# Single-query attention over 256 heads: a tile's maximum, weights and values are placed beside the next tile's product

## The chip, the cores and the metric

One NeuronCore of a Trainium2 chip. The metric is the time of one launch on the device in microseconds (us), as the median of several runs. TensorE is called PE here (its weight loads PEld), VectorE DVE, ScalarE ACT, GpSimd POOL and SyncE SP.

## What is computed

Eight batches of 32 heads, each with a single query row of 128 numbers, 4096 keys and 4096 values, all in bf16. Softmax is taken in full over the 4096 keys of each head.

```python
B, H, Sq, Skv, Dh = 8, 32, 1, 4096, 128
def reference(q, k, v):
    scale = q.shape[-1] ** -0.5
    scores = jnp.einsum('bhqd,bhkd->bhqk', q, k) * scale
    attn = _softmax(scores, axis=-1)
    return jnp.einsum('bhqk,bhkd->bhqd', attn, v)
```

K and V are 256 x 4096 x 128 x 2 bytes each, 537 MB together, and every byte of them is used once.

## The kernel before

The 256 heads go through the core in 64 tiles of four heads (G = 4). A tile of K or V is 128 partitions x 128 keys (C) x 128 numbers of d, 4 MB; 32 partitions hold one head. K and V tiles share one pool of five buffers (`kv_pool`, SLOTS = 5), and SP issues their loads (line 106), one transfer a tile, in the order k(t+1), v(t). A load waits until the tile that was in its buffer has been read for the last time. The last v alone is loaded in four pieces.

The work on tile t is in two functions. `scores_of(t)` first forms the product of K and the query on DVE, in place, in chunks of MC = 64 keys: a multiplication by the query (line 132), then an addition of the upper half of d onto the lower half (line 135), so two of each per tile. PE then sums the remaining 64 numbers of d into four per key, by 16 multiplications with the identity that accumulate in one PSUM bank `ps` (line 144). DVE reduces these four to one score (line 149), takes the maximum of the partition (line 153), spreads it over 32 columns (line 155), takes the extreme over the 32 partitions of the head (line 160) and adds it to a mask that keeps each head on its own partitions (line 164, `bias`). ACT forms the weights with four exponentials (line 170), one per head, with their sums; PE adds the sums over the partitions (`zp`, line 175), and DVE takes the reciprocal (`rz`, line 177).

`values_of(t)` multiplies the weights by V on PE, 32 multiplications into one PSUM bank `av` (line 187). ACT copies the result out (`comb`, line 192), PE puts the four parts of it together (`op`, line 195), and ACT scales it by `rz` (line 202). Eight tiles' results go out in one store (line 206).

Every fourth tile `q_prep` loads four tiles' queries from POOL (line 115), spreads them over the partitions on PE (line 117) and copies them on ACT (line 121).

The main loop calls `scores_of(t)`, then `values_of(t - 1)`. The kernel text gives no engine order by hand beyond the order of these calls: the instructions of an engine are put into a fixed stream when the program is built, and each engine works through its stream strictly in order. That stream need not be the order of the calls, as the rows below show. The score bank `ps`, the bank `av` and the weights `w` have two buffers each.

Of the kernel before, what the change touches and what calls it, by code (L numbers as in the profile page):

```python
# [11 lines left out]
F32 = mybir.dt.float32  # L12
# [7 lines left out]
def kernel(  # L20
# [10 lines left out]
    P = nc.NUM_PARTITIONS  # L31
# [3 lines left out]
    C = S // PH  # L35
    NT = NH // G
# [1 line left out]
    UC = 128  # L38
    DS = 512 // UC
    NU = C // UC  # L40
    MC = 64
    QN = 512 // D
    ON = 8
    CB = 4
# [10 lines left out]
    small = ctx.enter_context(tc.tile_pool(name="small", bufs=3))  # L55
# [40 lines left out]
    loads = {}  # L96

    def load(kind, t):
        src = k_t if kind == "k" else v_t
        buf = kv_pool.tile([P, C, D], BF16, name=f"{kind}t", tag="kv")  # L100
        cuts = [C]
        if kind == "v" and t == NT - 1:
            cuts = [C // 2, C // 4, C // 8, C // 8]
        c0 = 0
        for n in cuts:
            nc.sync.dma_start(buf[:, c0 : c0 + n, :], src[t, :, c0 : c0 + n, :])
            c0 += n
        loads[kind, t] = buf
# [3 lines left out]
    def q_prep(t):  # L112
        if t % QN == 0:
            qrow = q_pool.tile([G, QN, D], BF16, name="qrow", tag="qrow")
            nc.gpsimd.dma_start(qrow[:], q_g[:, t : t + QN, :])  # L115
            qp = ps_q.tile([P, QN * D], F32, name="qp", tag="qp")
            nc.tensor.matmul(  # L117
                qp[:], lhsT=sel[:], rhs=qrow.rearrange("g n d -> g (n d)"), start=True, stop=True
            )
            qb = q_pool.tile([P, QN, D], BF16, name="qb", tag="qb")  # L120
            nc.scalar.activation(out=qb.rearrange("p n d -> p (n d)"), in_=qp[:], func=ACT.Copy)  # L121
            qbs[t // QN] = qb

    state = {}

    def scores_of(t):
        kt = loads.pop(("k", t))
        qb = qbs[t // QN]
        j = t % QN
        for c0 in range(0, C, MC):  # L130
            part = kt[:, c0 : c0 + MC, :]
            nc.vector.tensor_tensor(  # L132
                out=part, in0=part, in1=qb[:, j : j + 1, :].to_broadcast([P, MC, D]), op=ALU.mult
            )
            nc.vector.tensor_tensor(  # L135
                out=part[:, :, 0 : D // 2], in0=part[:, :, 0 : D // 2],
                in1=part[:, :, D // 2 : D], op=ALU.add,
            )
        sc = small.tile([P, C], F32, name="sc", tag="sc")
        for u in range(NU):  # L140
            ps = ps_s.tile([P, UC, DS], F32, name="ps", tag="ps")
            n = D // 2 // DS
            for s in range(n):
                nc.tensor.matmul(  # L144
                    ps[:], lhsT=ident[:],
                    rhs=kt[:, u * UC : (u + 1) * UC, s * DS : (s + 1) * DS],
                    start=(s == 0), stop=(s == n - 1),
                )
            nc.vector.tensor_reduce(  # L149
                out=sc[:, u * UC : (u + 1) * UC], in_=ps[:], axis=AX.X, op=ALU.add  # L150
            )
        pmax = small.tile([P, 1], F32, name="pmax", tag="pmax")
        nc.vector.tensor_reduce(out=pmax[:], in_=sc[:], axis=AX.X, op=ALU.max)  # L153
        spread = small.tile([P, 32], F32, name="spread", tag="spread")
        nc.vector.tensor_scalar(  # L155
            out=spread[:], in0=zero[:], scalar1=pmax[:, 0:1], scalar2=-scale,
            op0=ALU.add, op1=ALU.mult,
        )
        nmax = small.tile([P, 1], F32, name="nmax", tag="nmax")
        nc.vector.tensor_reduce(  # L160
            out=nmax[:], in_=spread[:], axis=AX.X, op=ALU.min, apply_transpose=True
        )
        bias = small.tile([P, G], F32, name="bias", tag="bias")
        nc.vector.tensor_scalar(  # L164
            out=bias[:], in0=own[:], scalar1=nmax[:, 0:1], scalar2=None, op0=ALU.add
        )
        w = w_pool.tile([P, C, G], BF16, name="w", tag="w")
        esum = small.tile([P, G], F32, name="esum", tag="esum")
        for g in range(G):
            nc.scalar.activation(  # L170
                out=w[:, :, g], in_=sc[:], func=ACT.Exp, bias=bias[:, g : g + 1], scale=scale,
                accum_out=esum[:, g : g + 1],
            )
        zp = ps_z.tile([G, 1], F32, name="zp", tag="zp")
        nc.tensor.matmul(zp[:], lhsT=esum[:], rhs=ones[:], start=True, stop=True)  # L175
        rz = small.tile([G, 1], F32, name="rz", tag="rz")
        nc.vector.reciprocal(out=rz[:], in_=zp[:])  # L177
        state[t] = (w, rz)
# [3 lines left out]
    def values_of(t):  # L182
        w, rz = state.pop(t)
        vt = loads.pop(("v", t))
        av = ps_v.tile([CB * G, CB * D], F32, name="av", tag="av")
        for c0 in range(0, C, CB):
            nc.tensor.matmul(  # L187
                av[:], lhsT=w[:, c0 : c0 + CB, :], rhs=vt[:, c0 : c0 + CB, :],
                start=(c0 == 0), stop=(c0 == C - CB),
            )  # L190
        comb = small.tile([CB * G, CB * D], BF16, name="comb", tag="comb")
        nc.scalar.activation(out=comb[:], in_=av[:], func=ACT.Copy)  # L192
        op = ps_o.tile([G, D], F32, name="op", tag="op")
        for m in range(CB):
            nc.tensor.matmul(  # L195
                op[:], lhsT=ident[0 : CB * G, m * G : (m + 1) * G],
                rhs=comb[:, m * D : (m + 1) * D], start=(m == 0), stop=(m == CB - 1),
            )
        if t % ON == 0:
            stages[t // ON] = o_pool.tile([G, ON, D], BF16, name="stage", tag="stage")  # L200
        stage = stages[t // ON]
        nc.scalar.activation(out=stage[:, t % ON, :], in_=op[:], func=ACT.Copy, scale=rz[:, 0:1])  # L202
        if t == NT - 1 or t == NT - 2 or (t % ON == ON - 1):
            lo = {NT - 1: NT - 1, NT - 2: NT - ON}.get(t, t - ON + 1)
            eng = nc.scalar if t == NT - 1 else nc.gpsimd
            eng.dma_start(o_g[:, lo : t + 1, :], stage[:, lo % ON : t % ON + 1, :])
# [3 lines left out]
    for t in range(NT):  # L210
        if t + 1 < NT:
            load("k", t + 1)
        load("v", t)
        if t + 2 < NT:
            q_prep(t + 2)
        scores_of(t)
        if t > 0:
            values_of(t - 1)
    values_of(NT - 1)


# [28 lines left out]
```

## Time and profile before

| what | value |
|---|---|
| median of 3 runs | 1506.79 us (1506.4 to 1508.59) |
| the profiled execution, its own time | 1508.7 us |
| its span, first to last instruction | 1506.9 us |
| mean granted TensorE clock | 0.766 of full speed |
| DVE busy | 953.6 us, 63% of the span |
| PE busy | 893.4 us, 59% |
| K and V read | 537 MB, 356 GB/s over the span |

The profiled execution is 1.9 us longer than the median, and 1.8 us of its time lie outside the span. The profile page gives shares over the whole span; a stage's limit is read from the timeline and from what each engine waited for. Durations are in microseconds unless marked ns. Two neighbouring instructions of one engine can overlap by some ten ns in the records, and the ends of matrix multiplications are modelled.

### The profile page before, as it was taken

The numbers are of one execution on the slowest core, as the hardware profiler recorded it, in microseconds if no ns is written. First come the engines' busy times: TensorE is split into PE (matmuls) and PEld (weight loads), VectorE is DVE, ScalarE is ACT, GpSimd is POOL, SyncE is SP. The second block draws the span as 40 slices with busy tenths as digits, with TensorE's granted clock in tenths as the row PEclk, the third lists the DMA queues.
The fourth block names the chain that finished last, engine by engine and source line by source line (L and its number), as shares of the span: only waits on it lengthen the run. The fifth ranks groups of instructions, "written<-read, shape, count | busy, mean of one in ns | idle before, by whom it ended". The sixth has DMA issues, their size and how long they took to land.

```text
span 1506.9 us, 8736 instructions
## 1 busy us (share of the span) xinstructions
PE 893.4 (59%) x3472; PEld 326.9 (22%) x3472; DVE 953.6 (63%) x642; ACT 182.2 (12%) x657; POOL 15.7 (1%) x36
## 2 busy tenths in 40 slices
PE   2656556566475574665745647556566565564666
PEld 0212222122121221221212212222122122221222
DVE  6575675665756756657566576575665766756653
ACT  0111011111010110111101101011011110110111
POOL 1000000000000000000000000000000000000000
PEclk9777777787786876878778678687787787777878
DMA  9999898888988988889898898898888888888870
GB/s 403 431 432 392 352 378 354 379 347 349 391 336 361 376 348 377 355 342 389 329 383 362 335 402 344 341 392 346 376 361 347 379 350 358 378 349 377 348 321 1
DMA packets 19681, 537.58 MB, mean 357 GB/s; under 512 B 2776, under 2 KB 2844, under 8 KB 3128
## 3 DMA queue, kind: packets, MB, share of 16 engines
q1 hardware_dynamic: 18864, 536.88, 85.2%
q8 instruction: 27, 0.44, 0.1%
q0 software_dynamic: 768, 0.14, 0.1%
q14 instruction: 14, 0.11, 0.0%
q10 hardware_dynamic: 8, 0.00, 0.0%
HBM read 536.94 MB, written 0.07 MB: 356 GB/s over the span
## 4 chain that ended last, share of the span: by engine, by line
DVE 63%; PE 27%; ACT 7%; issue 1%; DMA 1%; ACTq 0%; DVEq 0%
DVE kt L132 37%; PE ps L144 25%; DVE kt L135 19%; ACT w L170 7%; DVE sc L149 3%; DVE pmax L153 1%; DVE spread L155 1%; DVE bias L164 1%; DVE nmax L160 1%; PE zp L175 1%; DMA kt<-in_k_dram 1%; PE av L187 1%; DVE rz L177 0%; ACTq L170 0%; PE op L195 0%
## 5 line engine op out<-in xcount | busy, mean ns | idle before, releaser
L144 PE MATMUL ps<-kt,ident 128*128 128x512 bf16 x1024 | 383.9, 554 | 473.2 <-DVE kt L135 473.2
L132 DVE TENSOR_TENSOR kt<-kt,qb 128x8192 bf16<-128x8192 bf16 x128 | 560.3, 4419 | 12.9 <-DMA kt<-in_k_dram 12.6
L187 PE MATMUL av<-vt,w 128*16 128x512 bf16 x2048 | 481.3, 384 | 0.0
L144 PEld LDWEIGHTS <-ident 128*128 128x128 bf16 x1024 | 132.8, 130 | 719.4 <-issue 701.3
L135 DVE TENSOR_TENSOR kt<-kt 128x4096 bf16<-128x4096 bf16 x128 | 287.1, 2283 | 0.0
L149 DVE TENSOR_REDUCE sc<-ps 128x128 f32<-128x512 f32 x64 | 44.2, 691 | 380.6 <-PE ps L144 380.6
L187 PEld LDWEIGHTS <-w 128*16 128x16 bf16 x2048 | 173.8, 90 | 325.8 <-issue 105.0
L170 ACT ACTIVATE w<-sc,bias 128x128 bf16<-128x128 f32 x256 | 110.8, 567 | 999.2 <-DVE bias L164 999.2
L177 DVE RECIPROCAL rz<-zp 4x1 f32<-4x1 f32 x64 | 9.9, 155 | 135.3 <-PE zp L175 135.3
L170 ACT ACTIVATION_READ_ACCUMULATOR w<-sc,bias 128x1 f32 x256 | 64.7, 253 | 0.0
L192 ACT ACTIVATE comb<-av 16x512 bf16<-16x512 f32 x64 | 37.6, 587 | 223.7 <-PE av L187 223.7
L117 PE MATMUL qp<-qrow,sel 4*128 4x512 bf16 x16 | 9.3, 583 | 83.5 <-ACT qb L121 68.2
L195 PE MATMUL op<-comb,ident 16*4 16x128 bf16 x256 | 24.2, 212 | 42.5 <-ACT comb L192 42.5
L195 PEld LDWEIGHTS <-ident 16*4 16x4 bf16 x256 | 16.8, 77 | 70.0 <-issue 70.0
L202 ACT ACTIVATE stage<-op,rz 4x128 bf16<-4x128 f32 x64 | 22.9, 358 | 30.0 <-PE op L195 30.0
L153 DVE TENSOR_REDUCE pmax<-sc 128x1 f32<-128x128 f32 x64 | 18.3, 286 | 2.1
L175 PE MATMUL zp<-ones,esum 128*4 128x1 f32 x128 | 12.3, 165 | 11.1 <-ACT w L170 11.0
L121 ACT ACTIVATE qb<-qp 128x512 bf16<-128x512 f32 x16 | 9.6, 597 | 68.3 <-DVE kt L132 58.8
L115 POOL DMA_DIRECT2D qrow<-in_q_dram x16 | 9.3, 581 | 798.9 <-PE qp L117 798.9
L155 DVE TENSOR_SCALAR spread<-zero,pmax 128x32 f32<-128x32 f32 x64 | 15.4, 241 | 2.3
L164 DVE TENSOR_SCALAR bias<-own,nmax 128x4 f32<-128x4 f32 x64 | 14.6, 229 | 2.4
L175 PEld LDWEIGHTS zp<-ones,esum 128*4 128x4 f32 x128 | 5.8, 84 | 43.6 <-ACT w L170 43.6
(18 smaller groups left out, 23.3 us busy)
## 6 DMA issues: line engine op xcount, KB each, us to landing
kt<-in_k_dram SPq DMA_DIRECT2D x64, 4096.0 KB, 15.0
vt<-in_v_dram SPq DMA_DIRECT2D x63, 4096.0 KB, 12.3
vt<-in_v_dram SPq DMA_DIRECT2D x1, 2048.0 KB, 10.1
vt<-in_v_dram SPq DMA_DIRECT2D x1, 1024.0 KB, 12.2
vt<-in_v_dram SPq DMA_DIRECT2D x2, 512.0 KB, 13.4
qrow<-in_q_dram POOLq DMA_DIRECT2D x16, 4.0 KB, 6.5
out_dram<-stage POOLq DMA_DIRECT2D x7, 8.0 KB, 6.6
out_dram<-stage POOLq DMA_DIRECT2D x1, 7.0 KB, 2.0
```

What stands on the lines that cost most here:

```text
L132: nc.vector.tensor_tensor(out=part, in0=part, in1=qb[:, j : j + 1, :].to_broadcast([P, MC, D]), op=ALU.mult)
L135: nc.vector.tensor_tensor(out=part[:, :, 0 : D // 2], in0=part[:, :, 0 : D // 2], in1=part[:, :, D // 2 : D], op=ALU.add,)
L144: nc.tensor.matmul(ps[:], lhsT=ident[:], rhs=kt[:, u * UC : (u + 1) * UC, s * DS : (s + 1) * DS], start=(s == 0), stop=(s == n - 1),)
L149: nc.vector.tensor_reduce(out=sc[:, u * UC : (u + 1) * UC], in_=ps[:], axis=AX.X, op=ALU.add)
L153: nc.vector.tensor_reduce(out=pmax[:], in_=sc[:], axis=AX.X, op=ALU.max)
L155: nc.vector.tensor_scalar(out=spread[:], in0=zero[:], scalar1=pmax[:, 0:1], scalar2=-scale, op0=ALU.add, op1=ALU.mult,)
L164: nc.vector.tensor_scalar(out=bias[:], in0=own[:], scalar1=nmax[:, 0:1], scalar2=None, op0=ALU.add)
L170: nc.scalar.activation(out=w[:, :, g], in_=sc[:], func=ACT.Exp, bias=bias[:, g : g + 1], scale=scale, accum_out=esum[:, g : g + 1],)
L175: nc.tensor.matmul(zp[:], lhsT=esum[:], rhs=ones[:], start=True, stop=True)
L187: nc.tensor.matmul(av[:], lhsT=w[:, c0 : c0 + CB, :], rhs=vt[:, c0 : c0 + CB, :], start=(c0 == 0), stop=(c0 == C - CB),)
L192: nc.scalar.activation(out=comb[:], in_=av[:], func=ACT.Copy)
L195: nc.tensor.matmul(op[:], lhsT=ident[0 : CB * G, m * G : (m + 1) * G], rhs=comb[:, m * D : (m + 1) * D], start=(m == 0), stop=(m == CB - 1),)
```

## The change

`scores_of` is cut into three functions: `product(t, lo, hi)` for the DVE work on a range of keys, `sum_over_d(t)` for the 16 PE multiplications, which now leaves its PSUM banks in the list `sums[t]`, and `weights_of(t)` for everything from the reduction of the four numbers (line 149 before) to `rz`. MC goes from 64 to 32, so a product is four multiplications of 128x4096 and four additions of 128x2048 instead of two and two of twice that size. The loop now calls the first half of the product of t, the weights of t-1, the second half of the product of t, the values of t-1, and the sum over d of t. No operation on the data is added or left out otherwise.

```diff
-    MC = 64
+    MC = 32
...
-    def scores_of(t):
-        kt = loads.pop(("k", t))
+    def product(t, lo, hi):
+        kt = loads["k", t]
         qb = qbs[t // QN]
         j = t % QN
-        for c0 in range(0, C, MC):
+        for c0 in range(lo, hi, MC):
             part = kt[:, c0 : c0 + MC, :]
...
-        sc = small.tile([P, C], F32, name="sc", tag="sc")
+
+    sums = {}
+
+    def sum_over_d(t):
+        kt = loads.pop(("k", t))
+        sums[t] = []
         for u in range(NU):
             ps = ps_s.tile([P, UC, DS], F32, name="ps", tag="ps")
...
+            sums[t].append(ps)
+
+    def weights_of(t):
+        sc = small.tile([P, C], F32, name="sc", tag="sc")
+        for u, ps in enumerate(sums.pop(t)):
             nc.vector.tensor_reduce(
                 out=sc[:, u * UC : (u + 1) * UC], in_=ps[:], axis=AX.X, op=ALU.add
             )
...
-        scores_of(t)
+        product(t, 0, C // 2)
+        if t > 0:
+            weights_of(t - 1)
+        product(t, C // 2, C)
         if t > 0:
             values_of(t - 1)
+        sum_over_d(t)
+    weights_of(NT - 1)
     values_of(NT - 1)
```

## Rows read from the trace of the kernel before

**Rows 1.** The page, first part: span, and busy time of each engine.
```profile
span 1506.9 us, 8736 instructions
...
PE 893.4 (59%) x3472; PEld 326.9 (22%) x3472; DVE 953.6 (63%) x642; ACT 182.2 (12%) x657; POOL 15.7 (1%) x36
```

**Rows 2.** The page, chain that ended last: shares of the span by engine.
```profile
DVE 63%; PE 27%; ACT 7%; issue 1%; DMA 1%; ACTq 0%; DVEq 0%
```

**Rows 3.** The waits of all engines: total us, times, longest us.
```profile
DVE sc L149 <- PE ps L144: 380.6, 63, 6.7
...
DVE rz L177 <- PE zp L175: 135.3, 64, 2.4
...
DVE kt L132 <- DMA kt<-in_k_dram: 12.6, 1, 12.6
```

**Rows 4.** Timeline of DVE, one tile in mid-span: start us, us, instructions.
```profile
606.82 0.69 DVE L149 TENSOR_REDUCE sc<-ps 128x128 f32<-128x512 f32 x1 [6.63 <-PE ps L144]
...
608.39 0.23 DVE L164 TENSOR_SCALAR bias<-own,nmax 128x4 f32<-128x4 f32 x1
...
610.73 0.16 DVE L177 RECIPROCAL rz<-zp 4x1 f32<-4x1 f32 x1 [2.11 <-PE zp L175]
610.81 8.76 DVE L132 TENSOR_TENSOR kt<-kt,qb 128x8192 bf16<-128x8192 bf16 x2
619.48 4.49 DVE L135 TENSOR_TENSOR kt<-kt 128x4096 bf16<-128x4096 bf16 x2
```

**Rows 5.** Timeline of PE, the same tile and the start of the next.
```profile
600.24 6.54 PE L144 MATMUL ps<-kt,ident 128*128 128x512 bf16 x16 [8.71 <-DVE kt L135]
606.71 3.62 PE L187 MATMUL av<-vt,w 128*16 128x512 bf16 x16
610.50 0.19 PE L175 MATMUL zp<-ones,esum 128*4 128x1 f32 x2 [0.17 <-ACT w L170]
610.55 3.40 PE L187 MATMUL av<-vt,w 128*16 128x512 bf16 x15
614.62 0.38 PE L195 MATMUL op<-comb,ident 16*4 16x128 bf16 x4 [0.67 <-ACT comb L192]
614.93 0.38 PE L187 MATMUL av<-vt,w 128*16 128x512 bf16 x1
624.02 4.91 PE L144 MATMUL ps<-kt,ident 128*128 128x512 bf16 x16 [8.71 <-DVE kt L135]
```

**Rows 6.** Timeline of DVE, the first two tiles.
```profile
26.70 8.75 DVE L132 TENSOR_TENSOR kt<-kt,qb 128x8192 bf16<-128x8192 bf16 x2
35.38 0.68 DVE L149 TENSOR_REDUCE sc<-ps 128x128 f32<-128x512 f32 x1
35.98 2.28 DVE L135 TENSOR_TENSOR kt<-kt 128x4096 bf16<-128x4096 bf16 x1
38.17 0.28 DVE L153 TENSOR_REDUCE pmax<-sc 128x1 f32<-128x128 f32 x1
38.37 2.28 DVE L135 TENSOR_TENSOR kt<-kt 128x4096 bf16<-128x4096 bf16 x1
...
51.26 0.15 DVE L177 RECIPROCAL rz<-zp 4x1 f32<-4x1 f32 x1 [2.05 <-PE zp L175]
```

**Rows 7.** Timeline of DVE, the last tile.
```profile
1488.24 0.69 DVE L149 TENSOR_REDUCE sc<-ps 128x128 f32<-128x512 f32 x1 [5.86 <-PE ps L144]
...
1492.16 0.16 DVE L177 RECIPROCAL rz<-zp 4x1 f32<-4x1 f32 x1 [2.11 <-PE zp L175]
```

**Rows 8.** The page, groups of instructions: busy us, mean ns of one, idle before.
```profile
L132 DVE TENSOR_TENSOR kt<-kt,qb 128x8192 bf16<-128x8192 bf16 x128 | 560.3, 4419 | 12.9 <-DMA kt<-in_k_dram 12.6
...
L135 DVE TENSOR_TENSOR kt<-kt 128x4096 bf16<-128x4096 bf16 x128 | 287.1, 2283 | 0.0
```

**Rows 9.** Busy time in two stretches; last: clock, DMA share, GB/s.
```profile
55.00:100.00 45.00, 28.03 (x103) 10.00 (x103) 27.24 (x21) 5.69 (x21) 0.57 (x1) 0.73 1.00 430
...
600.00:624.00 24.00, 14.23 (x54) 5.19 (x54) 15.09 (x11) 2.68 (x10) 0.00 (x0) 0.71 0.84 349
```

## The prediction

> **What bounds the kernel now.** I began with the busy times [rows 1]: no engine is above 63%, so the bound is a chain through several engines. The chain that ended last says which: DVE has 63% of it, PE 27%, ACT 7%, the loads 1% [rows 2]. The waits say where DVE hands over: it stands 380.6 us in 63 places before the reduction of the scores, until PE has summed over d (6.04 us each), and 135.3 us in 64 places before the reciprocal, until exponentials and `zp` are through (2.11 us each) [rows 3]. It waited for a K tile once, at the start [rows 3].
>
> One tile of the timeline shows this as a closed loop [rows 4, 5]. The reduction starts at 606.82, `bias` ends at 608.62, so the short chain of five takes 1.80 us; 2.11 us of waiting and 0.16 us of reciprocal follow; the product runs from 610.81 to 623.97, 13.2 us; then PE sums, for 4.91 to 6.54 us. The reciprocal of tile 1 is at 51.26 and that of tile 63 at 1492.16 [rows 6, 7], so 62 tiles took 1440.9 us, **23.24 us a tile**: 1.8 + 2.1 + 0.2 + 13.2 + 6.0, the parts just named.
>
> Are the loads near their limit? From 55 to 100 us, when five buffers were queued, they moved 430 GB/s at a DMA share of 1.00; in mid-span 349 GB/s at 0.84 [rows 9]. At 430 GB/s a tile's 8.39 MB take **19.5 us**: the floor under any gain.
>
> **The order of the streams.** The order of the calls is not the order in which an engine runs. In tile 1, DVE ran both multiplications of the product, the reduction of tile 0, an addition of tile 1, the maximum of tile 0, the other addition [rows 6]: where an instruction needs the one just ahead of it on DVE, another that was ready was put between. PE likewise begins one multiplication of the next values ahead of the next sum, splits the values around `zp`, and puts them before `zp` although the calls come after it [rows 5]. In mid-span nothing is filled into the short chain [rows 4], because before the change nothing else counted as ready there: the next K tile was evidently reckoned as landing later than the chip delivers it. In the changed kernel something is always ready beside the chain: the second half of the same tile's product. I therefore expect the stream reduction, mult, maximum, mult, spread, add, extreme, add, `bias`, and not the chain in one piece.
>
> **The change, part by part.**
> *Smaller chunks.* Four multiplications of 128x4096 and four additions of 128x2048. An instruction of 4096 took 2283 ns and one of 8192 4419 ns [rows 8]: 147 ns fixed and 0.52 ns an element. Four more instructions cost 0.6 us a tile if the fixed part is paid in full; the starts lie closer than the durations (two multiplications in 8.67 us, 610.81 to 619.48 [rows 4]), which leaves 65 ns of the 147 and 0.26 us. Half the product is then 6.7 to 6.9 us; I take 6.7, for the starts count in a full stream.
> *The wait for the sum over d* (6.04 us) gets cover on DVE: the first half of the next product. That is the gain intended. *The wait for the reciprocal* stays: it is still behind `bias`, and the product of the next tile is queued behind it on DVE. DVE's own work and this wait come to 13.5 + 1.8 + 2.1 + 0.2 = 17.6 us a tile, so DVE alone does not set the end.
> *What is late next.* The new loop runs from one reduction to the next through all three engines. Reduction to `bias` with four fillers: 1.8 + 6.7 = 8.5 us. `bias` to the first value multiplication: 608.62 to 610.55, 1.9 us [rows 4, 5]. The 32 value multiplications, now ahead of the sum by call: 15 take 3.40 us and 16 take 3.62 [rows 5], so 7.0 us at the 2.4 GHz level. `comb` and `op`: 0.67 + 0.38 = 1.05 us. The sum over d of the next tile: its product ends just before `bias`, so PE can begin it while the exponentials run, 4 or 5 multiplications in 1.9 us at 0.41 us each (6.54 over 16 [rows 5]); about 3 fit in the 0.67 us before `op`, 8 are left, at 0.21 us: 1.7 us. Together 8.5 + 1.9 + 7.0 + 1.05 + 1.7 = **20.2 us**, with gaps of some 30 ns between nine DVE instructions and the hand-overs 20.4.
> *The clock.* PE would idle about 8.5 us a tile, as it does now (8.71), and now each sum begins at the 1.2 GHz level and rises within it: 16 multiplications at 0.43 and 0.21 us fit 6.54 us with 6.2 us at the low level, 4.91 us with 3.0 [rows 5]. In the changed kernel about 2 us of that fall into the early part of the sum, which waits anyway; the remaining 1.0 to 4.2 us fall on the values and cost half their length, 0.5 to 2.1 us. I take 0.5, by the row with 4.91: the loop that ends with it (606.8 to 628.9, 22.1 us) is shorter than the mean of 23.24 and so the nearer one to the new loop. This is the weakest choice in the sum; with the mean of now (6.04 us for 16 [rows 3], 5.2 us at the low level) the cost would be 1.6, the loop 22.0 and the time 1432. With 0.5 the loop is **20.9 us**, 2.35 less than now, with 20.4 and 22.7 as its ends.
> *Loads.* A v load is still released by the sum, a k load by the end of the values; their order on SP stays, both now come within some 3 us of each other. 8.39 MB in 20.9 us is 401 GB/s, under the 430 seen, so they stay hidden, with 1.4 us to spare. POOL's query loads are not moved past anything that waits.
> *Head and tail.* Reduction 1 (at 47.4 now, 3.85 us ahead of 51.26 by the chain of rows 4) comes about 7 us later, since the values of tile 0 now stand before it; behind the last reduction the values of the tile before are gone, 18.7 us (1488.24 to 1506.9 [rows 1, 7]) become 14 to 15. Net +3 us.
>
> **The sum.** 62 x 2.35 - 3 = 143 us: span 1506.9 to 1364, execution 1508.7 to 1366, and against the median, which is 1.9 lower, **1364 us**. With loops of 20.4 and 22.7: 1334 and 1476.
>
> **The rivals.**
> *The chain stays in one piece, as the calls have it.* The loop through the engines loses the 6.7 us of fillers and is some 14 us, DVE needs 17.6, and the loads' 19.5 us decide: 537 MB at 430 GB/s is 1249 us, plus 3 before and some 25 behind the last load: 1277. Against it stand rows 6. Chance 0.15.
> *The reduction is put ahead of the next product,* so the change does not do what it says: DVE waits for the sum as now. Only the wait for the reciprocal goes (product before it), 2.1 less 0.3 for chunks: 21.4 us, 1396. Rows 4 have this order, but by calls that asked for it. Chance 0.08.
> *Slower: the whole sum lands behind the values.* If PE is given no multiplication of the sum ahead of `zp`, all 16 follow: 8.5 + 1.9 + 7.0 + 1.05 + 3.4 = 21.9, and with gaps 22.1 us; from 2.3 us at the low clock on, at half a microsecond lost for each, it is over 23.24. With the 5.2 us of now it is 24.7: 1507 + 62 x 1.5 + 3 = 1603. Against it: rows 5 show PE starting whatever is ready. Chance 0.07.
> *The loads are the bound already.* From 55 to 100 us 430 GB/s went with all engines at work [rows 9], and DVE waited for K once [rows 3]; were the 349 GB/s of mid-span the limit, nothing would change: 1507. Chance 0.02. The Trainium skill (DMA: Bandwidth & Descriptors, Where 436 GB/s comes from) says that some 358 GB/s of HBM bind a core's loads into SBUF; by that the 537 MB need 1500 us and the kernel is done. The 430 GB/s row speaks against that rule on this core.
>
> **How the numbers follow.** The forecast keeps 0.68. About 3 us, 0.2%, can be told from no change. Its ends lie between 1334 and 1476, almost all of it below 1440, with the second rival inside. The first rival lies below; to 1280 the range takes in half of it. Left out: the slower rival, the loads' rival, half the first and the worst clock, together under 0.2. So 1280 to 1440. Faster: 0.15 + 0.08 + 0.67 = 0.90; same 0.03; slower 0.07.
>
> **What would show it.** Right: DVE's stream with halves of the product between reduction, maximum, spread, extreme and `bias`; the wait before the reduction down from 6.0 to about 3 us (20.9 - 17.6), the one before the reciprocal still near 2; PE with a few sum multiplications, `zp`, 32 values, then the rest of the sum; K and V near 400 GB/s. Wrong: the chain in one piece with DVE waiting for K; a reduction that stands before the first multiplication; a loop above 23 us, or values spending most of their time at 1.2 GHz.

## The result, and the profile after

| | before | after |
|---|---|---|
| median | 1507.13 us (1506.4 to 1508.59, 4 runs) | 1395.3 us (1393.52 to 1396.14, 4 runs) |
| span of the profiled execution | 1506.9 us | 1391.7 us |
| mean granted TensorE clock | 0.766 | 0.807 |
| K and V over the span | 356 GB/s | 386 GB/s |

The ratio is 0.9255, with a 95% interval of 0.9239 to 0.9271: 112 us less. The forecast was 1364 us, 1280 to 1440.

The page of the changed kernel, its busy times and the shares of the chain that ended last (before: [rows 1, 2]):

```profile
PE 856.0 (62%) x3472; PEld 305.0 (22%) x3472; DVE 946.5 (68%) x898; ACT 182.3 (13%) x657; POOL 15.7 (1%) x36
...
PE 52%; DVE 38%; ACT 8%; issue 1%; DMA 1%; DVEq 0%; ACTq 0%
PE av L197 37%; DVE kt L132 21%; PE ps L149 13%; DVE kt L135 11%; ACT w L180 8%; DVE sc L159 3%; PE op L205 1%; DVE pmax L163 1%; DMA kt<-in_k_dram 1%; PE zp L185 1%; DVE bias L174 1%; DVE spread L165 1%; DVE nmax L170 1%; DVEq L159 0%; ACTq L180 0%
```

The same shares by line, in the kernel before:

```profile
DVE kt L132 37%; PE ps L144 25%; DVE kt L135 19%; ACT w L170 7%; DVE sc L149 3%; DVE pmax L153 1%; DVE spread L155 1%; DVE bias L164 1%; DVE nmax L160 1%; PE zp L175 1%; DMA kt<-in_k_dram 1%; PE av L187 1%; DVE rz L177 0%; ACTq L170 0%; PE op L195 0%
```

The chain has changed hands. DVE led it with 63%; now PE does with 52%, and the largest single item is the value multiplications (37%), which had 1% before. Half the product is still on it (21% + 11%, against 37% + 19%).

The waits of the changed kernel, DVE's three (before: [rows 3]; total us, times, longest us):

```profile
DVE sc L159 <- PE ps L149: 283.8, 63, 10.5
DVE rz L187 <- PE zp L185: 135.4, 64, 2.4
...
DVE kt L132 <- DMA kt<-in_k_dram: 12.4, 1, 12.4
```

The wait for the sum over d fell from 6.04 to 4.50 us a tile (283.8 over 63), and did not go. The wait ahead of the reciprocal is untouched, and DVE still waits for a K tile only once. The timeline of DVE in mid-span shows the stream (before: [rows 4]):

```profile
607.08 0.69 DVE L159 TENSOR_REDUCE sc<-ps 128x128 f32<-128x512 f32 x1 [3.82 <-PE ps L149]
607.69 2.28 DVE L132 TENSOR_TENSOR kt<-kt,qb 128x4096 bf16<-128x4096 bf16 x1
609.89 0.28 DVE L163 TENSOR_REDUCE pmax<-sc 128x1 f32<-128x128 f32 x1
610.08 1.22 DVE L135 TENSOR_TENSOR kt<-kt 128x2048 bf16<-128x2048 bf16 x1
611.22 0.23 DVE L165 TENSOR_SCALAR spread<-zero,pmax 128x32 f32<-128x32 f32 x1
611.36 2.28 DVE L132 TENSOR_TENSOR kt<-kt,qb 128x4096 bf16<-128x4096 bf16 x1
613.56 0.20 DVE L170 TRANSPOSE_TENSOR_REDUCE nmax<-spread 128x1 f32<-128x32 f32 x1
613.69 1.21 DVE L135 TENSOR_TENSOR kt<-kt 128x2048 bf16<-128x2048 bf16 x1
614.82 0.22 DVE L174 TENSOR_SCALAR bias<-own,nmax 128x4 f32<-128x4 f32 x1
617.16 0.15 DVE L187 RECIPROCAL rz<-zp 4x1 f32<-4x1 f32 x1 [2.11 <-PE zp L185]
...
629.37 0.69 DVE L159 TENSOR_REDUCE sc<-ps 128x128 f32<-128x512 f32 x1 [5.39 <-PE ps L149]
```

Between every two members of the short chain stands a piece of the second half of the next product. Reduction to the end of `bias` took 1.80 us before; here it takes 7.96 (607.08 to 615.04). The timeline of PE for the same tile and the start of the next (before: [rows 5]):

```profile
614.96 1.87 PE L149 MATMUL ps<-kt,ident 128*128 128x512 bf16 x4 [7.98 <-DVE kt L135]
616.93 0.19 PE L185 MATMUL zp<-ones,esum 128*4 128x1 f32 x2
616.98 9.16 PE L197 MATMUL av<-vt,w 128*16 128x512 bf16 x32
626.08 1.04 PE L149 MATMUL ps<-kt,ident 128*128 128x512 bf16 x4
627.04 0.38 PE L205 MATMUL op<-comb,ident 16*4 16x128 bf16 x4
627.36 1.90 PE L149 MATMUL ps<-kt,ident 128*128 128x512 bf16 x8
...
639.27 8.27 PE L197 MATMUL av<-vt,w 128*16 128x512 bf16 x32
```

PE sums with four multiplications at the low level of its clock while the exponentials run, then come `zp`, all 32 values, four more of the sum while ACT copies, `op`, and the last eight. The reduction waits for those eight. 32 values take 9.16 us in this tile and 8.27 in the next; at the 2.4 GHz level they took 3.40 + 3.62 = 7.0 [rows 5].

Two stretches of the changed kernel in mid-span (clock, DMA share and GB/s last; before: [rows 9]) show the loads nearer to their 430 GB/s, but not there:

```profile
600.00:622.00 22.00, 13.91 (x54) 4.85 (x53) 16.07 (x16) 2.68 (x10) 0.00 (x0) 0.77 0.97 404
622.00:644.00 22.00, 13.91 (x59) 4.99 (x57) 14.49 (x15) 2.68 (x10) 0.00 (x0) 0.77 0.91 380
```

### The profile page after: what moved, and what is told of

It reads as the page before. It is cut to its first block, busy times and chain, and to the rows that moved or that the text cites. A ratio compares the mean times of both kernels' runs of the same rounds, so it can differ in the third digit from the quotient of the medians.

```text
span 1391.7 us, 9050 instructions
## 1 busy us (share of the span) xinstructions
PE 856.0 (62%) x3472; PEld 305.0 (22%) x3472; DVE 946.5 (68%) x898; ACT 182.3 (13%) x657; POOL 15.7 (1%) x36
## 4 chain that ended last, share of the span: by engine, by line
PE 52%; DVE 38%; ACT 8%; issue 1%; DMA 1%; DVEq 0%; ACTq 0%
PE av L197 37%; DVE kt L132 21%; PE ps L149 13%; DVE kt L135 11%; ACT w L180 8%; DVE sc L159 3%; PE op L205 1%; DVE pmax L163 1%; DMA kt<-in_k_dram 1%; PE zp L185 1%; DVE bias L174 1%; DVE spread L165 1%; DVE nmax L170 1%; DVEq L159 0%; ACTq L180 0%
## 5 line engine op out<-in xcount | busy, mean ns | idle before, releaser
L132 DVE TENSOR_TENSOR kt<-kt,qb 128x4096 bf16<-128x4096 bf16 x256 | 577.6, 2275 | 12.4 <-DMA kt<-in_k_dram 12.4
L149 PE MATMUL ps<-kt,ident 128*128 128x512 bf16 x1024 | 308.3, 440 | 410.8 <-DVE kt L135 410.2
L197 PE MATMUL av<-vt,w 128*16 128x512 bf16 x2048 | 523.6, 420 | 0.0
L135 DVE TENSOR_TENSOR kt<-kt 128x2048 bf16<-128x2048 bf16 x256 | 305.1, 1210 | 0.0
L197 PEld LDWEIGHTS <-w 128*16 128x16 bf16 x2048 | 193.8, 97 | 299.1 <-issue 102.8
L149 PEld LDWEIGHTS <-ident 128*128 128x128 bf16 x1024 | 95.2, 103 | 666.9 <-issue 591.7
L159 DVE TENSOR_REDUCE sc<-ps 128x128 f32<-128x512 f32 x64 | 44.2, 691 | 283.8 <-PE ps L149 283.8
L205 PEld LDWEIGHTS <-ident 16*4 16x4 bf16 x256 | 12.4, 78 | 27.8 <-issue 27.8
## 6 DMA issues: line engine op xcount, KB each, us to landing
vt<-in_v_dram SPq DMA_DIRECT2D x2, 512.0 KB, 17.6
```

The costliest lines, as they stand in the source:

```text
L132: nc.vector.tensor_tensor(out=part, in0=part, in1=qb[:, j : j + 1, :].to_broadcast([P, MC, D]), op=ALU.mult)
L135: nc.vector.tensor_tensor(out=part[:, :, 0 : D // 2], in0=part[:, :, 0 : D // 2], in1=part[:, :, D // 2 : D], op=ALU.add,)
L149: nc.tensor.matmul(ps[:], lhsT=ident[:], rhs=kt[:, u * UC : (u + 1) * UC, s * DS : (s + 1) * DS], start=(s == 0), stop=(s == n - 1),)
L159: nc.vector.tensor_reduce(out=sc[:, u * UC : (u + 1) * UC], in_=ps[:], axis=AX.X, op=ALU.add)
L197: nc.tensor.matmul(av[:], lhsT=w[:, c0 : c0 + CB, :], rhs=vt[:, c0 : c0 + CB, :], start=(c0 == 0), stop=(c0 == C - CB),)
L205: nc.tensor.matmul(op[:], lhsT=ident[0 : CB * G, m * G : (m + 1) * G], rhs=comb[:, m * D : (m + 1) * D], start=(m == 0), stop=(m == CB - 1),)
```

## The experiments

Two theories stood against each other from the start. The **loop theory** is the forecast's: one tile costs the way from one reduction through the fillers, `bias`, the exponentials, the values and the rest of the sum to the next reduction, and a low PE clock on top. The **loads theory**: with 380 to 404 GB/s in mid-span the loads are near what they give, and the order on the engines matters little. A third, the **clock theory**, puts most of what lies above 20.4 us a tile down to the low clock.

### pinned: the short chain in one piece

```diff
+    def pin(ins):
+        return tc.keep_in_program_order(ins)
...
-            nc.vector.tensor_tensor(
+            pin(nc.vector.tensor_tensor(
...
-        nc.vector.reciprocal(out=rz[:], in_=zp[:])
-        state[t] = (w, rz)
+        state[t] = (w, zp)
...
         product(t, C // 2, C)
         if t > 0:
+            reciprocal_of(t - 1)
             values_of(t - 1)
```

Every DVE instruction of product, weights and reciprocal is pinned behind the one called before it.

> DVE's stream is pinned to the order of the calls: first half of the product of t, the short chain of t-1 in one piece from the reduction to bias, second half of the product of t, then the reciprocal of t-1, which moves from weights_of to just ahead of values_of. Loop theory (the time goes through reduction, fillers, bias, exponentials, values, rest of the sum): the 6.7 us of fillers leave the loop, which falls from 21.3 us to some 15 us and so below the 19.5 us of the loads at 430 GB/s; about 1280 us, 1265 to 1300, with DVE waiting for K tiles. Loads theory (the 380 to 404 GB/s seen now are all that the loads give beside this work): no change, 1395 us. Clock theory (most of the time above 20.4 us is the low PE clock, and the order hardly matters): 1340 to 1395 us.

Measured: **1276.92 us** (1276.84 to 1277.03), ratio to the kernel before 0.8471, interval 0.8458 to 0.8483. Timeline of DVE of this kernel:

```profile
606.47 0.15 DVE L194 RECIPROCAL rz<-zp 4x1 f32<-4x1 f32 x1
610.34 2.29 DVE L135 TENSOR_TENSOR kt<-kt,qb 128x4096 bf16<-128x4096 bf16 x1 [3.72 <-DMA kt<-in_k_dram]
...
617.27 0.69 DVE L162 TENSOR_REDUCE sc<-ps 128x128 f32<-128x512 f32 x1
...
618.83 0.23 DVE L177 TENSOR_SCALAR bias<-own,nmax 128x4 f32<-128x4 f32 x1
```

and its waits and the page's lines on loads:

```profile
DVE kt L135 <- DMA kt<-in_k_dram: 244.9, 62, 12.4
```

```profile
GB/s 401 434 430 427 431 433 431 428 430 432 431 432 429 430 431 431 429 432 429 432 431 431 430 430 431 430 432 430 431 431 429 431 432 430 431 433 429 430 427 97
```

With the chain back at 1.8 us (617.27 to 619.06) the reduction hardly waits any more (9.4 us in 2 places), DVE waits for a K tile in 62 places, and the loads run at some 430 GB/s from the second slice to the last but one. The loop theory gave the size; the loads theory falls, for the changed kernel at least, and so does the clock theory as priced here (1340 to 1395). This is the first rival of the prediction, made to happen, and at its price of 1277 us. It is also the fastest kernel of the study, and what holds it is the loads. How long its loop through the engines is (some 15 us by the expectation) is therefore not seen, only that it is under 19.5.

### pinned_rz: the same with the reciprocal behind bias

```diff
+        if t > 0:
+            reciprocal_of(t - 1)
         product(t, C // 2, C)
         if t > 0:
-            reciprocal_of(t - 1)
             values_of(t - 1)
```

> The pinned stream with the reciprocal back where the calls of the change have it, right behind bias, ahead of the second half of the product: DVE waits 2.1 us there again. Loop theory: DVE needs 13.6 + 1.8 + 2.1 + 0.2 = 17.7 us a tile, still under the 19.5 us of the loads; 1275 to 1282 us, with DVE's wait for K tiles shorter by 2.1 us. If moving the reciprocal was what made the pinned kernel fast: above 1300 us.

Measured: 1277.73 us (1276.51 to 1278.12), ratio 0.8474 (0.8462 to 0.8487). Its waits:

```profile
DVE rz L194 <- PE zp L188: 135.1, 64, 2.1
DVE kt L135 <- DMA kt<-in_k_dram: 110.5, 61, 12.4
```

The 135 us of waiting for `zp` are back, and 134 us of waiting for K are gone (244.9 to 110.5). Moving the reciprocal is worth nothing where the loads decide. This kernel makes the same calls in the same order as the changed one and differs from it in the pins alone, so the order of DVE's stream did it all.

### rz_late: the wait ahead of the reciprocal taken out of the changed kernel

```diff
-        product(t, 0, C // 2)
+        half = product(t, 0, C // 2)
+        if t > 1:
+            with tc.issue_after(half):
+                reciprocal_of(t - 2)
+            scale_of(t - 2)
```

> The changed kernel with the reciprocal of tile t-2 (and the scaling by it) put behind the first half of the product of t, where zp is long done: DVE's wait of 2.11 us ahead of the reciprocal goes. Loop theory: that wait is beside the loop, and the wait ahead of the reduction grows by the same 2.1 us; 1390 to 1400 us. If DVE's waits were what costs: 62 times 2.1 us less, 1265 us, or 1280 by the loads.

Measured: 1395.58 us (1394.28 to 1395.87), ratio 0.9256 (0.9242 to 0.927), the changed kernel's own. Its wait for the sum:

```profile
DVE sc L160 <- PE ps L150: 420.7, 63, 10.7
```

420.7 less 283.8 is 136.9: the whole wait moved to the place ahead of the reduction. A wait of 135 us in the list cost nothing.

### mc64: longer fillers

```diff
-    MC = 32
+    MC = 64
```

> The changed kernel with MC = 64 again. The stream has one addition, one multiplication and one addition of the double size between reduction and bias: fillers of 2.2 + 4.4 + 2.2 = 8.8 us in place of 6.7. Loop theory: the loop grows by some 2 us to about 23.3 us, 1500 to 1530 us, though four instructions a tile are gone. Instruction cost alone: 0.28 us a tile saved, 1378 us. Loads theory: 1395 us.

Measured: **1554.85 us** (1553.85 to 1555.12), ratio 1.0313 (1.0298 to 1.0329): slower than the kernel before, and 25 us above what the loop theory gave. Timeline of DVE, two reductions and the `bias` between:

```profile
603.48 0.69 DVE L159 TENSOR_REDUCE sc<-ps 128x128 f32<-128x512 f32 x1 [7.26 <-PE ps L149]
...
613.40 0.23 DVE L174 TENSOR_SCALAR bias<-own,nmax 128x4 f32<-128x4 f32 x1
...
627.43 0.69 DVE L159 TENSOR_REDUCE sc<-ps 128x128 f32<-128x512 f32 x1 [7.21 <-PE ps L149]
```

Reduction to the end of `bias` is 10.15 us, 2.2 more than with MC = 32, as the fillers say. The mean loop is 23.89 us (54.27 to 1535.44, 62 loops), 2.6 more; the other 0.4 lie in the values, from their first multiplication to the next instruction on PE 8.5 us a tile in the mean, against 8.1 with MC = 32. So without the smaller chunks the change as it is called would have lost time, with four instructions a tile fewer.

### before_mc32: the smaller chunks alone

```diff
-    MC = 64
+    MC = 32
```

in the kernel before.

> The kernel before with MC = 32, nothing else: what the smaller chunks cost by themselves where the product lies on the path. Four more instructions a tile at 65 to 147 ns: 0.26 to 0.6 us a tile, 1524 to 1545 us.

Measured: 1504.87 us (1503.91 to 1506.73), ratio 0.9984 (0.9975 to 0.9993): not 17 to 38 us slower, but 2.5 faster, a difference just clear of the noise. DVE's waits in it:

```profile
DVE sc L149 <- PE ps L144: 359.6, 63, 6.5
```

The product did grow, by 0.28 us, from 13.16 (610.81 to 623.97 [rows 4]) to 13.44. But the wait for the sum shrank from 6.04 to 5.71 us a tile (359.6 over 63). The sum begins at the low clock and ends at the high one, and here less of it ran low: the mean granted clock is 0.781, against 0.766. The expectation left that out.

### sum_first: the sum called ahead of the values

```diff
         product(t, C // 2, C)
+        sum_over_d(t)
         if t > 0:
             values_of(t - 1)
-        sum_over_d(t)
```

> sum_over_d(t) is called ahead of values_of(t-1), nothing else. DVE's stream then has the whole short chain of t-1 ahead of the product of t, and PE's has the whole sum ahead of the values. Loop theory: no half of the product covers the sum over d any more; 13.4 us of product, 1.8 of chain, 0.2 of reciprocal and 5 to 6.5 of the sum make 20.4 to 21.9 us, 1340 to 1430 us. By the calls alone (the sum is done early, so nothing waits for it): the loads' 19.5 us, about 1280 us. Loads theory: 1395 us.

Measured: 1426.29 us (1424.74 to 1427.74), ratio 0.9461 (0.9445 to 0.9477). Timeline of DVE:

```profile
600.66 0.69 DVE L159 TENSOR_REDUCE sc<-ps 128x128 f32<-128x512 f32 x1 [5.54 <-PE ps L149]
...
602.23 0.23 DVE L174 TENSOR_SCALAR bias<-own,nmax 128x4 f32<-128x4 f32 x1
602.37 4.49 DVE L132 TENSOR_TENSOR kt<-kt,qb 128x4096 bf16<-128x4096 bf16 x2
...
621.27 0.69 DVE L159 TENSOR_REDUCE sc<-ps 128x128 f32<-128x512 f32 x1 [5.42 <-PE ps L149]
...
627.88 0.15 DVE L187 RECIPROCAL rz<-zp 4x1 f32<-4x1 f32 x1 [4.82 <-PE zp L185]
```

This is the second rival of the prediction: the chain in one piece, but ahead of the whole product, so that nothing covers the sum. Such a loop takes 20.6 us (600.66 to 621.27), inside the 20.4 to 21.9 expected. Its time is at the upper end because the reciprocal waits in 15 places, up to 4.8 us, as at 627.88, where it stands ahead of the whole product; every fourth loop, up to that of tile 51, takes 26.4 us. It is each time the loop behind the one in which PE spreads a new set of queries (line 117); why the reciprocal's place in the stream changes there is not shown. That the sum is early by the calls does not help: the stream, not the call, decides.

### warm28, warm16, warm36: PE kept at work

The loop's parts at the 2.4 GHz level, from the rows above: 7.96 to `bias`, 1.94 to the values, 7.0 for them, 1.3 to the last eight of the sum, 2.0 for those, 20.2 us in all; the mean loop is 21.31 (54.02 to 1375.08, 62 loops). Is the clock the rest? The expectation for 28 takes 6.8 us for the values and so 20.0 in all; warm36 shows 7.0.

```diff
+        wp = ps_w.tile([P, 512], F32, name="wp", tag="wp")
+        with tc.issue_after(mm.ins):
+            for i in range(28):
+                x = nc.tensor.matmul(
+                    wp[:], lhsT=ident[:], rhs=junk[:], start=(i == 0), stop=(i == 28 - 1)
+                )
+        warm[t] = x.ins
```

with 28, 16 and 36 in turn; `mm` is the last multiplication of the sum, and the first of the next sum is ordered behind `warm[t]`.

> The changed kernel with 28 multiplications of zeros by the identity into a bank of their own on PE, behind the last multiplication of each sum and ahead of the first of the next (ps_o gives one of its two banks for it). The output does not use them. They fill 6 of the 8 us in which PE now stands idle. Clock theory of what the forecast missed: the loop of 21.3 us is 20.0 us of parts at the 2.4 GHz level (8.0 reduction to bias, 1.9 to the values, 6.8 values, 1.0 to op, 0.3 op, 1.9 rest of the sum) and 1.3 us of low clock; with PE kept at work the loop falls to about 20.0 to 20.3 us, 1315 to 1335 us. If the low clock is not what is missing, PE only has more to do: 1395 us or, where the multiplications run at the low level and outlast the idle time, above 1450 us.

> The same with 16 multiplications of zeros, 3.4 us of the 8 us; PE still stands idle for 4.6 us. Clock theory: between the two, 1320 to 1395 us, and where it lies shows how much of the idle time has to be filled. Otherwise as for 28.

> The changed kernel with 36 multiplications of zeros a tile in place of 28: 7.7 us at the 2.4 GHz level, which fills all but 0.2 us of the idle time ahead of the sum that 28 left (1.94 us of 8.1); only 0.95 us ahead of zp stay idle. If the remaining idle time is what lets the clock fall in one tile of four or five: the loop is 20.2 us in nearly all tiles, 1325 to 1335 us. If the clock falls regardless of it: 1380 us or more, with the values of one tile in four or five at 10 us.

Measured: 28 gave 1388.09 us (1383.77 to 1393.45), ratio 0.9211 (0.9181 to 0.924); 16 gave 1395.41 (1393.68 to 1397.16), ratio 0.9256 (0.9243 to 0.927); 36 gave **1325.77** (1325.66 to 1326.06), ratio 0.8792 (0.8777 to 0.8806). The expectation for 28 was missed by more than 50 us, and the timeline of PE with 28 says where:

```profile
629.01 1.02 PE L153 MATMUL ps<-kt,ident 128*128 128x512 bf16 x4 [1.94 <-DVE kt L138]
630.98 0.19 PE L204 MATMUL zp<-ones,esum 128*4 128x1 f32 x2 [0.95 <-ACT w L199]
631.03 7.07 PE L216 MATMUL av<-vt,w 128*16 128x512 bf16 x32
...
651.23 10.00 PE L216 MATMUL av<-vt,w 128*16 128x512 bf16 x32
```

Most tiles run their values in 7.07 us, but about every fourth takes 10.00 and the next 8.7: the clock still falls. With 16 nothing was gained (1320 to 1395 us expected), though the mean granted clock rose from 0.807 to 0.884: the values still run in 9.16, 8.27, 7.82 and 7.59 us in turn, as in the changed kernel. A mean clock over the span does not say what the clock costs. That kernel also has the one bank less, and its time shows that this costs nothing.

With 36 the 1.94 us of idle time shrink to 0.2, and a tile of PE's timeline and the view of clocks of that kernel read

```profile
606.23 1.02 PE L153 MATMUL ps<-kt,ident 128*128 128x512 bf16 x4 [0.22 <-DVE kt L138]
608.20 0.19 PE L204 MATMUL zp<-ones,esum 128*4 128x1 f32 x2 [0.94 <-ACT w L199]
608.25 7.07 PE L216 MATMUL av<-vt,w 128*16 128x512 bf16 x32
615.25 1.04 PE L153 MATMUL ps<-kt,ident 128*128 128x512 bf16 x4
```

```profile
core 0: 1324.3 us, clock 1.000
```

with a loop of 20.21 us (52.85 to 1305.75, 62 loops) against parts of 20.2. So the low clock costs the changed kernel 1395.3 - 1325.8 = 69.5 us, 1.1 us a tile. It lies on the values: to the next instruction on PE they take 7.0 us here (608.25 to 615.25), and 8.1 in the mean of the changed kernel. The expectation for 28 was wrong in taking 28 for enough to keep the clock up, not in what the clock costs.

## Why the prediction was right or wrong

**What bounds the kernel** held: a loop through three engines, no single one. pinned shows the floor of 19.5 us a tile where the prediction put it (19.46 from 51.93 to 1258.58, 62 loops).

**The order of the streams** held, but for two fillers in the other order than written: reduction, mult, maximum, add, spread, mult, extreme, add, `bias`. That inference from [rows 6] carries the whole forecast: pinned_rz, with nothing changed but that order, is 118 us faster. That is the least that the fillers cost, for there the loads decide. The change as called would have been worth 230 us; the fillers kept half of it. Why the stream is built so (the prediction has the next K tile reckoned as landing late) no run shows.

**Smaller chunks:** 0.26 us was the right end of the range (0.28 measured), but it is no loss in either kernel: before_mc32 gives it back through the clock, and in the changed kernel it shortens the fillers, which mc64 prices at 160 us.

**The wait for the reciprocal** stays and costs nothing, as costed; rz_late shows it.

**What is late next** was right in every place: 8.5 us forecast to `bias` (7.96), 1.9 (1.94) to the values, 7.0 (7.0 at the high level, in warm36), 1.05 (1.28) to the last eight, 1.7 (2.01) for them. With hand-overs 20.4 forecast, 20.2 by the rows and in warm36.

**The clock** is the step that failed, in size only. The prediction took 0.5 us from the better of two rows and called it its weakest choice; warm36 puts it at 1.1 us, between that and the mean of now (1.6). The better row was not typical: its loop (22.1 us) is the shortest of a pattern of five that repeats, told of in the last section. The parts came out 0.2 us a tile under the forecast and the clock 0.6 over it, so that some of the miss was hidden by luck. The upper loop of the range was also added up too long: 20.4 + 2.1 is 22.5 us, not 22.7, and 1464 us, not 1476. The loop is 21.31 us, not 20.9: 62 times 0.4 is 25 of the 28 us that the span lies above its 1364; the tail behind the last reduction, 16.6 us (1375.08 to 1391.7) against 14 to 15, is most of the rest.

**The signs named ahead:** the wait before the reduction was to be 3 us and is 4.5. Against 20.9 - 17.6 = 3.3, 0.4 us of that is the longer loop and 0.8 DVE's own work, which with the wait for the reciprocal takes 16.8 us (21.31 - 4.50) and not 17.6. The loads were to reach 400 GB/s and reach 386. Head: the first loop's reduction was to come 7 us later and comes 6.6 later (54.02 against 47.4).

**The rivals:** the chain in one piece and the reduction ahead of the product were both made and stand at 1277 and 1426 us, against 1277 and 1396 forecast. The 1396 is also where the changed kernel landed (1395.3): the time alone would have fitted that rival, and only DVE's stream, with the product woven into the chain, rules it out. The slower rival, with the whole sum behind the values, did not come about and was not tried with the fillers in place. That the loads were the bound already falls with pinned, which reads 421 GB/s over its span. The rule of the Trainium skill quoted with it (DMA: Bandwidth & Descriptors, Where 436 GB/s comes from) falls there too, for one core alone. Another page of the Trainium skill (HBM Reference, Specifications (TRN2)) says that a core streaming alone measures about 425 GB/s, and pinned agrees within about 2%: 427 to 434 in its full slices.

## What to carry to other kernels

Calling work in an order that overlaps is not yet an overlap: read from the trace in which order each engine really runs, and look above all for a short chain of dependent instructions with long independent ones woven into it, for each of those is then on the path. Price a wait only after asking what waits next to it: 135 us before the reciprocal were worth nothing, and 1.8 us of chain stretched to 8 were worth at least 118. Such fillers should be short, if they can't be kept out. Where a loop alternates PE work with idle time, take the clock's share from many tiles and not from one, and from the work that runs low on the path, not from the mean clock.

## What the runs showed of the hardware that was not expected

The low clock makes the loop settle into a pattern. In the kernel before, the distance between reductions repeats as 22.15, 23.01, 23.44, 23.67, 23.78 us; in the changed one as 22.29, 21.39, 20.94, 20.71. From one tile to the next what changes is halved (23.01 to 23.44, 0.43; to 23.67, 0.23; to 23.78, 0.11), as it would be if half of every microsecond at the low level were lost and the rise did not move with the loop. The starts of the sum's multiplications in the kernel before bear that out: they are 0.43 us apart before the rise and 0.22 behind it, and the rise comes 23.88 us behind the one before it in three loops of five, though the loops are 23.0 to 23.7 us long. Why it keeps that distance, and why it falls back (to 20.65 us) once in the pattern, is left open. Queries too are spread on PE every fourth tile, but they do not make the changed kernel's pattern of four: it goes on behind the last of them, and in the kernel before it has five. One effect is that 0.28 us more product a tile (before_mc32) came out as 0.07 us less loop (23.17 against 23.24).

Idle time of PE as short as 1.9 and 0.95 us stood ahead of a value stretch that fell to the low level in about every fourth tile of warm28, at a cost of 3 us in that tile, and ahead of others that did not; in warm36, with 0.2 and 0.95 us, the granted clock is 1.000 over the span. Why one tile of four and not each is left open.
